# Sparse attention and soft mixture of experts on one core: order of layer 2's weight loads, of the coefficient transposes and of the output blocks changed

## The chip, the core and the metric

The kernel runs on one core of one Trainium2 chip. The metric is device microseconds of one execution. One core has five engines that run side by side: TensorE (PE, with its weight loads shown as PEld), VectorE (DVE), ScalarE (ACT), GpSimd (POOL) and SyncE (SP). Sixteen DMA engines move data between the chip's memory and the core; nearly all of their transfers are issued by SP's queue, in the order in which they are written.

## What is computed

Attention over 8 batches, 8 heads, 576 positions and 64 columns with two sparse masks gives tokens `x` of 4608 x 512. A soft mixture of 8 experts with 4 slots each follows:

```python
logits = x @ phi                                  # 4608 x 32
slot_input = softmax(logits, over tokens).T @ x   # 32 x 512
for e in range(8):
    h = np.maximum(slot_input[e] @ w1[e], 0.0)    # layer 1: 4 x 1024
    slot_out[e] = h @ w2[e]                       # layer 2: 4 x 512
c = softmax(logits, over slots)                   # the coefficients
out = c @ slot_out                                # 4608 x 512, f32, 9.4 MB
```

`w1` and `w2` are 16.8 MB each, in f32.

## The kernel before, in words

The attention and the slot sums fill the first 180 us, in an order written out by hand (`ORDER`); the change leaves that part as it is. What follows is layer 1, layer 2 and the output.

**Weights.** `load_weights` issues 64 loads of 512 KB on SP's queue. Number 0 to 31 are layer 1's. Layer 2's are 32 to 63, in pairs of a group of four experts and a quarter of the hidden size (`GM`). Pairs 0 to 5 (32 to 55) are loaded whole, four loads each, every partition reading 4 KB in one run. Pairs 6 and 7 are loaded in halves of the output columns: 56 to 59 hold their left halves, 60 to 63 their right halves, read in runs of 1 KB (the view `128x4x256`). `seq` is the order of issue. The late loads go into buffers of layer 1's weights that TensorE has finished with.

**Layer 1.** `emit_first` (steps P0 to P6 of `ORDER`) and `emit_end1` (step "e") multiply one group of four experts and a quarter of the input at a time. `COEFF` says which coefficient work follows a step: `emit_cT` and `emit_cU` are PE transposes of `lall`, `emit_cV` is ACT's copy back, `emit_cA`, `emit_cE` and `emit_cB` are the softmax on DVE and ACT. The nine blocks of tokens are in three sets (0 to 3, 4 to 6, 7 and 8).

**Layer 2 and output.** A string of letters, `SEQ`, sets the order of the rest on all engines. "h" turns the hidden rows (`emit_hT`). "l" adds one pair to the left sum (output columns 0 to 255), "r" one pair to the right sum (`emit_l2`): 8 matmuls, 16 passes. "s" copies a finished sum to `acc` (`emit_sg`: first DVE, then ACT), "t" adds it up over row groups (`emit_rs`: two matmuls and a copy each by DVE and ACT to `x9b`). "o" and "O" write two blocks of tokens in the left and the right half of the columns (`emit_half`: 8 matmuls, 4 copies, 4 stores of 256 KB in runs of 1 KB), "f" writes one block in all columns (`emit_full`, runs of 2 KB). Each of the three is 1.05 MB of output. An "o" needs the left sum, an "O" and an "f" both sums. Before, `SEQ` closes the left sum, starts the right one in the waits of "s" and "t", writes three left blocks between the other right pairs, and then, after the right sum, three right blocks and three whole ones.

Of the kernel before, what the change touches and what calls it, by code (L numbers as in the profile page):

```python
# [28 lines left out]
NWX = 2  # L29
# [49 lines left out]
s9w s9P sw w.14 ac1 zz.15 w.15 sP0 sD0 P0 sP1 sD1 P1 zD zP rg P2 P3 P4 P5 P6  # L79
""".split()  # L80

SEQ = "eehhllllllllsrtrorrorrorrstOOOfff"


def shape_constants():
# [23 lines left out]
def tile_sparse_attention_soft_moe(  # L109
# [107 lines left out]
    def take():  # L217
        x = min(freed, key=lambda x: freed[x])
        del freed[x]
        return banks[x], x  # L220
# [11 lines left out]
    order = wbufs + [t[:, 1024 * k:1024 * k + 1024] for t, k in places]  # L232

    NL = len(order)
    seq = list(range(32 - NWX)) + list(range(32, NL)) + list(range(32 - NWX, 32)) + list(range(NL, 64))
    wts = {}

    reuse = [x for x in range(32) if x not in (3, 4, 5)]
# [6 lines left out]
    def load_weights(n):  # L245
        for _ in range(n):
            if len(wts) >= 64:
                return
            j = seq[len(wts)]
            buf = order[len(wts)] if j < NL else wts[reuse[j - NL]]  # L250
            wts[j] = buf
            if j < 32:

                g, r = divmod(j, 16)
                c, e = divmod(r, 4)
                nc.sync.dma_start(out=buf, in_=w1[4 * g + e, 128 * CH[c]:128 * CH[c] + 128, :])
            else:
                r = j - 32
                if r < 4 * NG:
                    (g, m), e = GM[r // 4], r % 4  # L260
                    src = w2[4 * g + e, 256 * m:256 * m + 256, :].rearrange("(p j) d -> p (j d)", j=2)
                    nc.sync.dma_start(out=buf, in_=src)
                else:

                    x, r = divmod(r - 4 * NG, 16 - 2 * NG)
                    g, m = GM[NG + r // 2]
                    src = w2[4 * g:4 * g + 4, 256 * m:256 * m + 256].rearrange("e (p j) d -> j p e d", j=2)[r % 2, :, :, 256 * x:256 * x + 256]
                    nc.sync.dma_start(out=buf.rearrange("p (e d) -> p e d", d=256), in_=src)
# [428 lines left out]
    fns = {}  # L697
# [150 lines left out]
    def emit_l1(g, c, xs):  # L848
        for x in xs:
            for e in range(4):  # L850
# [3 lines left out]

    COEFF = {2: ((emit_cA, 0), (emit_cE, 0)),
             3: ((emit_cA, 1), (emit_cE, 1), (emit_cB, 0)),
             4: ((emit_cT, 2), (emit_cA, 2), (emit_cE, 2), (emit_cB, 1)),
             5: ((emit_cU, 0), (emit_cV, 0), (emit_cB, 2)),
             6: ((emit_cU, 1), (emit_cV, 1), (emit_cU, 2), (emit_cV, 2))}

    def emit_first(n):
        if n == 0:
            ph.append(take())
        emit_l1(n // 4, n % 4, (0, 1))
        load_weights((3, 2, 4, 4, 4, 1, 0)[n])

        for fn, x in COEFF.get(n, ()):
            fn(x)
        if n == 1:
            for t in hts:  # L870
                nc.gpsimd.memset(t, 0.0)
# [20 lines left out]
    for a in range(2):  # L892
        r = slice(64 - 64 * a, 128 - 64 * a)
# [23 lines left out]
    for x in ORDER:  # L917
        if x in once:
            once[x]()
        elif x[0] == "w":  # L920
            load_weights(1)
        else:
            n, i = x.split(".")
            i = int(i)
            if n == "C2":
                emit_late(i)
            fns[n](i)
# [24 lines left out]
    free = [wts[j] for j in list(range(22, 32)) + list(range(32, 48))]  # L952
    pos = [take() for x in range(2)]

    def emit_l2(x, n):
        g, m = GM[n]
        for j in range(2):
            for e in range(4):
                if n < NG:
                    w = wts[32 + 4 * n + e][:, 512 * j + 256 * x:512 * j + 256 * x + 256]  # L960
                else:
                    w = wts[32 + 4 * NG + (16 - 2 * NG) * x + 2 * (n - NG) + j][:, 256 * e:256 * e + 256]
                nc.tensor.matmul(out=pos[x][0][32 * e:32 * e + 32, 0:256], lhsT=hts[g][:, 2 * m + j, 32 * e:32 * e + 32], rhs=w,  # L963
                                 start=(n == 0 and j == 0), stop=(n == 7 and j == 1), skip_group_check=True)

    rss = [None, None]
    def emit_sg(x):
# [46 lines left out]
    def emit_full(vb):  # L1014
# [15 lines left out]
        emit_out(po, store)  # L1030


    steps = {
        "l": (emit_l2, 0, iter(range(8))), "r": (emit_l2, 1, iter(range(8))),
        "o": (emit_half, 0, iter(range(3))), "O": (emit_half, 1, iter(range(3))), "f": (emit_full, iter((8, 6, 7))),
        "s": (emit_sg, iter(range(2))), "t": (emit_rs, iter(range(2))), "h": (emit_hT, iter(range(2))),
        "e": (emit_end1, iter(range(2))),
    }
    for step in SEQ:
        fn, *args = steps[step]  # L1040
# [31 lines left out]
```

## Time and profile before

| | us |
|---|---|
| median of 3 runs (243.9 to 248.25) | 245.46 |
| the profiled execution | 242.59 |
| its span, first to last instruction | 240.8 |
| PE busy, share of the span | 89% |
| DMA queue of SP, share of 16 engines | 92.2% |

The profile shows one execution. PE is busy nearly throughout, and so are the DMA engines, so the shares alone don't tell the bound; the last 60 us have to be read stretch by stretch. In a row of stretches, PE to POOL are busy microseconds, then come TensorE's granted clock as a share of full speed, the mean busy share of the 16 DMA engines (packets can overlap, so it may pass 1) and what they moved in GB/s.

### The profile page before, as it was taken

Reading aid. Unit: us, or ns where it says so; the run is one execution under the profiler, and the core shown is the slowest. Engines: PE = TensorE matmul, PEld = TensorE weight load, DVE = VectorE, ACT = ScalarE, POOL = GpSimd, SP = SyncE. Lnnn points to the kernel's source line nnn. Section 1 sums busy time; section 2 is a strip of 40 time slices with the busy share of each in tenths; the row PEclk is TensorE's granted clock in tenths of the full one; section 3 lists DMA queues with packets and bytes.
Section 4 is the critical chain, followed back from the end, with each engine's and each line's share of the span. In section 5 each row is a group of like instructions: output and inputs, shape, how many; then the busy total and the mean of one; then the engine's idle time right before and its main releaser. Section 6 shows DMA issues by size and latency. Waiting matters only on the chain.

```text
span 240.8 us, 9926 instructions
## 1 busy us (share of the span) xinstructions
PE 215.2 (89%) x4096; PEld 169.0 (70%) x4096; DVE 165.6 (69%) x381; ACT 154.3 (64%) x347; POOL 86.0 (36%) x189
## 2 busy tenths in 40 slices
PE   8899998998889999999999999899889999998700
PEld 3688897888778998897889898687753246455400
DVE  6097997896599978887977786799872831145900
ACT  2789898786769889878697988666440241135700
POOL 5466835626443271743327434733102000000000
PEclk9999999999999999999999999999999999999975
DMA  5987999989997998899999899999998999887996
GB/s 151 351 231 238 301 282 279 302 207 318 304 321 218 299 317 236 263 344 297 318 367 340 233 280 335 316 284 358 349 344 338 395 377 312 293 287 257 381 399 260
DMA packets 69597, 72.73 MB, mean 302 GB/s; under 512 B 32896, under 2 KB 59664, under 8 KB 69552
## 3 DMA queue, kind: packets, MB, share of 16 engines
q1 hardware_dynamic: 69184, 71.84, 92.2%
q8 instruction: 32, 0.52, 0.9%
q0 software_dynamic: 80, 0.15, 0.2%
q10 hardware_dynamic: 288, 0.11, 0.2%
q14 instruction: 13, 0.11, 0.2%
HBM read 62.65 MB, written 9.44 MB: 299 GB/s over the span
## 4 chain that ended last, share of the span: by engine, by line
PE 54%; DMA 18%; DVE 13%; issue 4%; ACT 3%; POOL 2%; SPq 1%; DVEq 0%; POOLq 0%; ACTq 0%
PE bank L340 10%; PE bank L390 7%; PE bank L470 7%; DMA natb<-in_q_dram 6%; PE bank L851 6%; DMA vs<-in_v_dram 5%; PE bank L518 4%; DMA wb<-in_moe_w_dram 4%; PE bank L963 3%; PE bank L462 3%; PE bank L276 2%; PE bank L988 2%; DVE xnb L500 2%; DMA natb<-in_k_dram 2%; PE bank L549 2%
## 5 line engine op out<-in xcount | busy, mean ns | idle before, releaser
L340 PE MATMUL bank<-cf,natb 128*128 128x128 f32 x276 | 40.2, 277 | 3.0 <-DMA natb<-in_k_dram 1.3
L340 PEld LDWEIGHTS bank<-cf,natb 128*128 128x128 f32 x276 | 30.8, 141 | 8.0 <-issue 3.0
L356 ACT COPY kLb<-bank 64x256 f32<-64x256 f32 x64 | 25.8, 403 | 7.5 <-PE bank L340 4.7
L427 DVE TENSOR_TENSOR pb<-bank,cb 128x512 f32<-128x512 f32 (+2 forms) x48 | 21.7, 472 | 11.4 <-PE bank L390 7.4
L500 DVE TENSOR_TENSOR xnb<-bank,rz 128x512 f32<-128x512 f32 (+1 forms) x33 | 21.6, 669 | 7.6 <-PE bank L470 4.9
L330 POOL COPY vb<-vb 64x1024 f32<-64x1024 f32 x16 | 16.7, 1041 | 25.8 <-DMA vb<-in_v_dram 14.8
L390 PE MATMUL bank<-kLb,qtb 128*32 128x128 f32 x576 | 23.1, 274 | 0.8 <-POOL kLb L383 0.8
L442 DVE TENSOR_REDUCE rz<-pb 128x10 f32<-128x640 f32 (+1 forms) x32 | 21.6, 684 | 1.0 <-ACT pb L439 0.6
L466 ACT COPY ptb<-bank 128x512 f32<-128x512 f32 x32 | 19.0, 598 | 4.5 <-PE bank L462 2.9
L432 DVE TENSOR_REDUCE mx<-pb 128x10 f32<-128x640 f32 (+1 forms) x32 | 21.5, 685 | 0.5
L435 DVE TENSOR_TENSOR pb<-pb,mx 128x640 f32<-128x640 f32 (+1 forms) x32 | 21.1, 673 | 0.3
L439 ACT ACTIVATE pb<-pb 128x640 f32<-128x640 f32 (+1 forms) x32 | 18.6, 597 | 3.5 <-DVE pb L435 3.3
L335 POOL COPY natb<-natb 128x512 f32<-128x512 f32 x15 | 9.6, 638 | 30.1 <-DMA natb<-in_q_dram 18.9
L462 PE MATMUL bank<-cf,pb 128*128 128x128 f32 x128 | 19.4, 276 | 0.8 <-ACT d L619 0.7
L518 PE MATMUL bank<-cf,xnb 128*128 128x128 f32 x128 | 18.8, 277 | 0.7 <-DVE xnb L500 0.5
L390 PEld LDWEIGHTS bank<-kLb,qtb 128*32 128x32 f32 x576 | 17.1, 110 | 3.4 <-POOL kLb L383 1.5
L364 ACT COPY kSb<-bank 64x512 f32<-64x512 f32 x32 | 18.6, 581 | 0.4
L387 POOL COPY kSb<-qtb 64x32 f32<-64x32 f32 x64 | 17.5, 273 | 2.4
L470 PE MATMUL bank<-vs,ptb 128*32 128x128 f32 x480 | 16.0, 274 | 2.4 <-DMA vs<-in_v_dram 1.1
L470 PE MATMUL bank<-vb,ptb 128*32 128x128 f32 x512 | 17.4, 274 | 0.0
L331 POOL COPY vb<-vb 64x1024 f32<-64x1024 f32 x16 | 16.8, 1048 | 0.7
L518 PEld LDWEIGHTS bank<-cf,xnb 128*128 128x128 f32 x128 | 14.4, 141 | 2.6 <-issue 1.2
(199 smaller groups left out, 457.2 us busy)
## 6 DMA issues: line engine op xcount, KB each, us to landing
wb<-in_moe_w_dram SPq DMA_DIRECT2D x48, 512.0 KB
natb<-in_k_dram SPq DMA_DIRECT2D x30, 256.0 KB
natb<-in_q_dram SPq DMA_DIRECT2D x30, 256.0 KB
vb<-in_v_dram SPq DMA_DIRECT2D x32, 144.0 KB
vs<-in_v_dram SPq DMA_DIRECT2D x30, 144.0 KB
out_dram<-wb SPq DMA_DIRECT2D x16, 256.0 KB
vb<-in_moe_w_dram SPq DMA_DIRECT2D x4, 512.0 KB
xnb<-in_moe_w_dram SPq DMA_DIRECT2D x3, 512.0 KB
```

Of the source, the lines that this page charges most:

```text
L340: nc.tensor.transpose(out=t[0][:, 128 * n:128 * n + 128], in_=src[:, 128 * n:128 * n + 128], identity=ident)
L356: ACT(out=dst.rearrange("d (p j n) -> d p j n", j=2, n=2)[:, :, :, n], in_=t[0][64 * n:64 * n + 64].rearrange("d (h j p) -> d p j h", j=2, ...
L390: nc.tensor.matmul(out=t[0][32 * c:32 * c + 32, x:x + wd], lhsT=lhsT, rhs=rhs, start=True, stop=True, skip_group_check=True)
L427: nc.vector.tensor_tensor(out=dst, in0=src, in1=masks[w].unsqueeze(1).unsqueeze(3).to_broadcast([P, n, kk, 2]), op=ALU.add)
L432: nc.vector.tensor_reduce(out=part(box[i][0], w), in_=psg[w].rearrange("p s k a -> p s a k"), op=ALU.max, axis=AX.X)
L435: nc.vector.tensor_tensor(out=psg[w], in0=psg[w], in1=over(box[i][0], w), op=ALU.subtract)
L442: nc.vector.tensor_reduce(out=part(box[i][1], w), in_=psg[w].rearrange("p s k a -> p s a k"), op=ALU.add, axis=AX.X)
L462: nc.tensor.transpose(out=t[0][:, 128 * r:128 * r + 128], in_=pb[:, lo + 128 * r:lo + 128 * r + 128], identity=ident)
L466: ACT(out=ptL if s == "L" else ptS, in_=t[0])
L470: nc.tensor.matmul(out=t[0][32 * c:32 * c + 32, 128 * r:128 * r + 128], lhsT=lhsT, rhs=rhs, start=True, stop=True, skip_group_check=True)
L500: nc.vector.tensor_tensor(out=xn[:, place(i, s), r0:r0 + nr].rearrange("p r (a d) -> p r a d", a=2), in0=t[0][:, 128 * r0:128 * r0 + 128 * ...
L518: nc.tensor.transpose(out=t[0][:, 128 * r:128 * r + 128], in_=xn[:, place(i, s), r, :], identity=ident)
```

## The change

Five things change together. `seq` issues loads 56 to 59 (the left halves of pairs 6 and 7) ahead of 48 to 55 (the whole pairs 4 and 5); each load's buffer follows its place in the order. The left sum takes its pairs in the same order (`LEFT`), and closes with pair 5. The coefficient work of sets 1 and 2 leaves layer 1's steps P4 to P6 and stands in `SEQ` as "T" and "A" around the second "h", and as "U" and "V" around "t". The right sum no longer has pairs in the waits of "s" and "t"; the first "o" follows "V". And all blocks of tokens but the ninth are written in halves: four "o" between the right pairs, then four "O" and one "f".

```diff
--- before.py
+++ after.py
@@ -79,7 +79,7 @@
 s9w s9P sw w.14 ac1 zz.15 w.15 sP0 sD0 P0 sP1 sD1 P1 zD zP rg P2 P3 P4 P5 P6
 """.split()
 
-SEQ = "eehhllllllllsrtrorrorrorrstOOOfff"
+SEQ = "eehThAllllllllsUtVorrorrorrorrstOOOOf"
 
 
 def shape_constants():
@@ -232,7 +232,7 @@
     order = wbufs + [t[:, 1024 * k:1024 * k + 1024] for t, k in places]
 
     NL = len(order)
-    seq = list(range(32 - NWX)) + list(range(32, NL)) + list(range(32 - NWX, 32)) + list(range(NL, 64))
+    seq = list(range(32 - NWX)) + list(range(32, NL)) + list(range(32 - NWX, 32)) + list(range(NL, 48)) + list(range(56, 60)) + list(range(48, 56)) + list(range(60, 64))
     wts = {}
 
     reuse = [x for x in range(32) if x not in (3, 4, 5)]
@@ -246,8 +246,8 @@
         for _ in range(n):
             if len(wts) >= 64:
                 return
-            j = seq[len(wts)]
-            buf = order[len(wts)] if j < NL else wts[reuse[j - NL]]
+            j, n = seq[len(wts)], len(wts)
+            buf = order[n] if n < NL else wts[reuse[n - NL]]
             wts[j] = buf
             if j < 32:
 
@@ -854,9 +854,8 @@
 
     COEFF = {2: ((emit_cA, 0), (emit_cE, 0)),
              3: ((emit_cA, 1), (emit_cE, 1), (emit_cB, 0)),
-             4: ((emit_cT, 2), (emit_cA, 2), (emit_cE, 2), (emit_cB, 1)),
-             5: ((emit_cU, 0), (emit_cV, 0), (emit_cB, 2)),
-             6: ((emit_cU, 1), (emit_cV, 1), (emit_cU, 2), (emit_cV, 2))}
+             4: ((emit_cB, 1),),
+             5: ((emit_cU, 0), (emit_cV, 0))}
 
     def emit_first(n):
         if n == 0:
@@ -952,6 +951,9 @@
     free = [wts[j] for j in list(range(22, 32)) + list(range(32, 48))]
     pos = [take() for x in range(2)]
 
+    LEFT = (0, 1, 2, 3, 6, 7, 4, 5)
+    LAST = LEFT[-1], 7
+
     def emit_l2(x, n):
         g, m = GM[n]
         for j in range(2):
@@ -961,7 +963,7 @@
                 else:
                     w = wts[32 + 4 * NG + (16 - 2 * NG) * x + 2 * (n - NG) + j][:, 256 * e:256 * e + 256]
                 nc.tensor.matmul(out=pos[x][0][32 * e:32 * e + 32, 0:256], lhsT=hts[g][:, 2 * m + j, 32 * e:32 * e + 32], rhs=w,
-                                 start=(n == 0 and j == 0), stop=(n == 7 and j == 1), skip_group_check=True)
+                                 start=(n == 0 and j == 0), stop=(n == LAST[x] and j == 1), skip_group_check=True)
 
     rss = [None, None]
     def emit_sg(x):
@@ -1030,9 +1032,15 @@
         emit_out(po, store)
 
 
+    def emit_c(*fns):
+        for fn, x in fns:
+            fn(x)
+
     steps = {
-        "l": (emit_l2, 0, iter(range(8))), "r": (emit_l2, 1, iter(range(8))),
-        "o": (emit_half, 0, iter(range(3))), "O": (emit_half, 1, iter(range(3))), "f": (emit_full, iter((8, 6, 7))),
+        "T": (emit_c, (emit_cT, 2)), "A": (emit_c, (emit_cA, 2), (emit_cE, 2), (emit_cB, 2)),
+        "U": (emit_c, (emit_cU, 1), (emit_cV, 1)), "V": (emit_c, (emit_cU, 2), (emit_cV, 2)),
+        "l": (emit_l2, 0, iter(LEFT)), "r": (emit_l2, 1, iter(range(8))),
+        "o": (emit_half, 0, iter(range(4))), "O": (emit_half, 1, iter(range(4))), "f": (emit_full, iter((8,))),
         "s": (emit_sg, iter(range(2))), "t": (emit_rs, iter(range(2))), "h": (emit_hT, iter(range(2))),
         "e": (emit_end1, iter(range(2))),
     }
```

PE at the close of the left sum, before: the last two rows of the right sum's first half pair, then the sum over row groups (`acc` by `cf`), the second half pair, and the first left block (`x9b` by `lall`). Buffers `wb_92` and `wb_93` are the turned hidden rows, the other operand is a weight buffer.

```order
L963 MATMUL bank_119<-qtb,wb_92 32x256
L963 MATMUL bank_119<-vs,wb_92 32x256
L978 MATMUL bank_124<-acc,cf 128x128
L978 MATMUL bank_118<-acc,cf 128x128
L963 MATMUL bank_119<-vs,wb_93 32x256
L963 MATMUL bank_119<-vb,wb_93 32x256
L963 MATMUL bank_119<-natb,wb_93 32x256 x2
L963 MATMUL bank_119<-vs,wb_93 32x256
L963 MATMUL bank_119<-vb,wb_93 32x256
L963 MATMUL bank_119<-natb,wb_93 32x256 x2
L988 MATMUL bank_121<-x9b,lall 128x256
```

The same place now: the last rows of the left sum, then the coefficient transposes (`lall` by `cf`) on both sides of the sum over row groups, then the first left block.

```order
L965 MATMUL bank_120<-wb_102,wb_92 32x256
L965 MATMUL bank_120<-wb_103,wb_92 32x256
L965 MATMUL bank_120<-wb_104,wb_92 32x256
L833 MATMUL bank_123<-cf,lall 128x128 x3
L980 MATMUL bank_121<-acc,cf 128x128
L980 MATMUL bank_125<-acc,cf 128x128
L833 MATMUL bank_118<-cf,lall 128x128 x2
L990 MATMUL bank_119<-x9b,lall 128x256
```

Two pairs of the right sum have left this place; five transposes have come in, and the first left block stands directly behind them.

SP's queue, layer 2's last loads, as a difference: buffers 90 to 96 now take the left halves (1 KB runs), buffers 101 to 104 a whole pair (4 KB runs).

```order
-L262 DMA wb_90<-in_moe_w_dram 128x1024
-L262 DMA wb_94<-in_moe_w_dram 128x1024
-L262 DMA wb_95<-in_moe_w_dram 128x1024
-L262 DMA wb_96<-in_moe_w_dram 128x1024
+L268 DMA wb_90<-in_moe_w_dram 128x4x256
+L268 DMA wb_94<-in_moe_w_dram 128x4x256
+L268 DMA wb_95<-in_moe_w_dram 128x4x256
+L268 DMA wb_96<-in_moe_w_dram 128x4x256
 L262 DMA wb_97<-in_moe_w_dram 128x1024
 L262 DMA wb_98<-in_moe_w_dram 128x1024
 L262 DMA wb_99<-in_moe_w_dram 128x1024
 L262 DMA wb_100<-in_moe_w_dram 128x1024
```

The four small-run loads have moved ahead by eight places; behind them now come the two whole pairs, and behind those, as before, the right halves in `wb_105` to `wb_108`.

PE in layer 1, between step P6 and the last step, as a difference: five coefficient transposes are gone from here.

```order
 L851 MATMUL bank_125<-wb_114,pb 32x512
 L851 MATMUL bank_125<-wb_115,pb 32x512
-L833 MATMUL bank_124<-cf,lall 128x128 x3
-L833 MATMUL bank_118<-cf,lall 128x128 x2
 L851 MATMUL bank_121<-wb_116,pb 32x512
 L851 MATMUL bank_121<-wb_117,pb 32x512
```

Layer 1's last products now follow step P6 directly.

## Rows read from the trace of the kernel before

**Rows 1.** The page's first part: span, busy time of each engine

```profile
span 240.8 us, 9926 instructions
...
PE 215.2 (89%) x4096; PEld 169.0 (70%) x4096; DVE 165.6 (69%) x381; ACT 154.3 (64%) x347; POOL 86.0 (36%) x189
```

**Rows 2.** Busy time by stretch: us, PE, PEld, DVE, ACT, POOL, clock, DMA share, GB/s

```profile
184.00:196.90 12.90, 12.90 (x113) 4.15 (x109) 8.05 (x22) 2.92 (x7) 1.84 (x2) 1.00 1.02 399
196.90:203.00 6.10, 6.03 (x90) 3.48 (x85) 0.85 (x2) 2.11 (x4) 0.00 (x0) 1.00 1.03 326
203.00:206.20 3.20, 2.77 (x52) 1.42 (x44) 0.00 (x0) 0.00 (x0) 0.00 (x0) 1.00 0.99 258
```

**Rows 3.** Busy time by stretch, before and after the last left load's landing

```profile
196.90:206.20 9.30, 8.80 (x136) 4.90 (x128) 0.85 (x2) 2.11 (x4) 0.00 (x0) 1.00 1.01 302
206.20:212.10 5.90, 5.87 (x92) 3.28 (x92) 1.87 (x4) 1.61 (x4) 0.00 (x0) 1.00 0.69 237
```

**Rows 4.** Chain of work that ended last, in order of time: start, us, what

```profile
196.25 9.94 DMA wb<-in_moe_w_dram
...
206.23 1.50 PE bank L963 x24
...
209.38 1.08 PE bank L988 x16
210.45 1.86 PE bank L963 x32
...
216.33 1.91 PE bank L963 x32
218.26 0.30 DVE acc L969
...
219.43 0.28 ACT x9b L979
219.75 2.04 PE bank L988 x32
```

**Rows 5.** Order of time on PE: start, us, line, out<-in, count [idle before it]

```profile
190.32 0.44 PE L794 MATMUL bank<-cf,lall 128*128 128x128 f32 x2
...
192.54 0.66 PE L833 MATMUL bank<-cf,lall 128*128 128x128 f32 x4
...
194.98 0.76 PE L833 MATMUL bank<-cf,lall 128*128 128x128 f32 x5
...
199.08 0.40 PE L963 MATMUL bank<-kSb,wb 128*32 128x256 f32 x1
...
206.23 0.64 PE L963 MATMUL bank<-wb,wb 128*32 128x256 f32 x8 [0.47 <-DMA wb<-in_moe_w_dram]
...
209.31 1.15 PE L988 MATMUL bank<-x9b,lall 32*128 32x256 f32 x16
```

**Rows 6.** Busy time by stretch, from the weights' end to the span's end

```profile
209.00:212.10 3.10, 3.10 (x56) 1.66 (x48) 1.29 (x2) 1.07 (x2) 0.00 (x0) 1.00 0.40 140
...
221.00:222.60 1.60, 1.60 (x24) 0.94 (x20) 1.60 (x3) 1.60 (x4) 0.00 (x0) 1.00 0.01 3
222.60:231.20 8.60, 4.43 (x60) 2.99 (x56) 5.64 (x10) 4.71 (x9) 0.00 (x0) 1.00 1.09 382
231.20:238.40 7.20, 0.00 (x0) 0.00 (x0) 0.00 (x0) 0.00 (x0) 0.00 (x0) 0.51 1.06 406
238.40:240.80 2.40, 0.00 (x0) 0.00 (x0) 0.00 (x0) 0.00 (x0) 0.00 (x0) 0.50 0.11 40
```

**Rows 7.** Order of time on ACT: coefficient copies of sets 1 and 2

```profile
195.57 0.75 ACT L838 COPY lall<-bank 128x384 f32<-128x384 f32 x2 [1.75 <-PE bank L833]
```

**Rows 8.** Order of time on DVE: the first copy of the left sum

```profile
206.94 0.29 DVE L969 COPY acc<-bank 128x128 f32<-128x128 f32 x1 [7.25 <-PE bank L963]
```

**Rows 9.** Order of time on SP's queue: first store of the first left block

```profile
211.24 0.39 SPq L1010 DMA_DIRECT2D out_dram<-wb  x1
```

**Rows 10.** Order of time on SP's queue: first store after the right sum

```profile
221.69 0.37 SPq L1010 DMA_DIRECT2D out_dram<-wb  x1
```

## The prediction

> **What bounds the kernel now.** I read the page first: PE is busy for 215.2 of 240.8 us [rows 1], which only says that the last 60 us must be read by stretches. The chain of waits names who holds up the end. One piece of 9.94 us is a weight load that lands at 206.19; the left sum's last matmuls follow it, then the right sum and the left blocks, all on PE, and from 221.8 on copies and stores [rows 4]. Up to 206.2 the DMA engines never rest (share 1.02, 1.03, 0.99), and the loads get slower as their runs get shorter: 399 GB/s while nearly all are in 4 KB runs, then 326 and 258 while the eight loads in 1 KB runs are on their way [rows 2]. Behind the weights the stretches show two pauses: 209.0 to 212.1 with share 0.40 (1.9 us idle) and 221.0 to 222.6 with 0.01 (1.6 us). After 222.6 the stores run at 382 and 406 GB/s to 238.4, and 2.4 us at 40 GB/s end the span [rows 6].
>
> So three things stand in a row. The left sum closes by DMA: its last eight passes start on the landing and end at 206.23 + 0.64 = 206.87 [rows 5]. The right sum then closes by PE at 216.33 + 1.91 = 218.24 [rows 4]. From there the stores drain by DMA. The change touches all three, and I cost them one by one against this execution: span 240.8, time 242.59, so 1.8 around the span. The median of the runs shown is 245.46, 1.2% above it; I scale by that at the end.
>
> **The left sum's close.** In layer 1, transposes of 0.44 and 0.76 us leave PE (the four of 0.66 stay), and the 0.44 comes back as "T" between the two turns of the hidden rows. Layer 2, which starts at 199.08, can so start 0.8 sooner, at 198.3 [rows 5]. That alone gains nothing: PE already waits for the last load (0.47 idle, released by the DMA [rows 5]). But it sets a floor. Two pairs take 1.86 us [rows 4], so eight pairs take 7.44 and PE could close the left sum at 205.7 at the earliest. The DVE and ACT work of "A" (half a dozen operations) falls under layer 2, where DVE sits idle for 7.25 us [rows 8]; I cost it at nothing.
>
> The landing decides. Before and after, the same loads must land before the left sum closes, four of them in 1 KB runs; only their order differs, and the DMA engines are busy throughout, so by bytes nothing changes. Two bounds come from rows. For the better: after 206.2 the engines still moved 5.9 us x 237 GB/s = 1.40 MB [rows 3], although the four right halves are 2.10 MB. So 0.70 MB of these had moved before the last left load was complete, worth 2.3 us at 302 GB/s [rows 3]: the 16 engines are not in step. If they were, the landing would be at 203.9, and PE's floor of 205.7 would decide. For the worse: the small-run loads may run at 258 instead of 326 GB/s where they now stand, 2.10 MB x (1/258 - 1/326) = 1.7 us later. I take 0.7 us earlier, nearest to rows 2: the 3.2 us just before the landing ran at 258 instead of 326, which cost 3.2 x (1 - 258/326) = 0.7 us, and now 4 KB runs stand there, with the right halves behind them.
>
> The Trainium skill, "DMA: Bandwidth & Descriptors", section "Why a DMA increments its semaphore by 16 and not by 1", says that a transfer runs on up to 16 engines that finish independently, and that only the full count means all data has landed. By that the lag of the slowest engine stays whatever is queued, the landing moves by nothing and the sum below would give 242.5 instead of 241.8 (rival 3); the 0.70 MB that moved ahead of the landing agree with the page, while no row shows whether the lag shrinks under larger runs.
>
> After the landing there is a little more to do. A left half needs only its own 8 passes at the end (0.64 us [rows 5]). The last load of a whole pair serves both halves of the hidden rows, so its one matmul and the four of the second half follow: half a round of a pair more, at most 0.93/2, I take 0.4. The left sum closes at 206.87 - 0.7 + 0.4 = 206.6 (205.7 to 209.0).
>
> **From the left sum to the right sum.** Before, the first left block starts at 209.31 [rows 5], 2.4 us after the close, because two right pairs fill the waits. Without pairs the same waits are seen after the right sum: closed at 218.24, first block at 219.75, 1.5 us [rows 4]. Now U and V lie there: five transposes (0.76 us on PE [rows 5]) and two ACT copies (0.75 in all [rows 7]). The first block queues behind V on PE, and its `x9b` copy queues behind U's copy on ACT. In the 1.5 us PE waits for a DVE copy of 0.30 and an ACT copy of 0.28 [rows 4], and DVE's part of the work stays ahead of ACT's, so most of both fits beside them; I take 0.1 for what shows; the other end is all of it, 1.5. That gives 1.6. Then come four blocks of 1.08 and eight pairs of 0.93 [rows 4]: 4.3 + 7.4. The right sum closes at 206.6 + 1.6 + 11.8 = 219.9, 1.7 us later than before: a fourth block and two pairs that had filled waits now stand in its way.
>
> **The drain.** From the right sum's close to the first bytes of the next stores it takes 222.6 - 218.24 = 4.4 us [rows 4, 6], unchanged: 224.3. Then five blocks are left instead of six. A block is 1.05 MB: 2.75 us in 1 KB runs (382 GB/s), 2.58 in 2 KB runs (406) [rows 6]. Before: 3 x 2.75 + 3 x 2.58 = 16.0. Now 4 x 2.75 + 2.58 = 13.6, so 2.4 less. The end: 224.3 + 13.6 + 2.2 = 240.1, where the same sum for before gives 222.6 + 16.0 + 2.2 = 240.8. Net: -0.3 (close) + 2.0 (path to the right sum) - 2.4 (drain) = -0.7 us. 241.8 on this execution's scale, 0.3% less; 244.7 on the median's.
>
> The pauses go where this says. The first store follows the first left block by 211.24 - 209.31 = 1.9 us [rows 5, 9], so it is issued at 206.6 + 1.6 + 1.9 = 210.1 instead of 211.24, about when the weights run out: the first pause mostly closes. The second stays. Left blocks come every 1.86 + 1.08 = 2.94 us [rows 4], slower than the DMA takes them, so the fourth one's bytes end near 222.6 and the next start at 224.3. What is late next is the right sum, by PE alone.
>
> **The rivals.** (1) *The left sum closes as early as PE allows*, because the engines draw level under the 4 KB runs. For it: PE's floor of 205.7. Against it: nothing in the trace shows the lag shrinking. 0.9 us better than the forecast: 240.9, 243.8 on the median's scale. (2) *Slower: the small-run loads cost more ahead of the whole pairs.* They ran at 326 GB/s in one stretch and at 258 in the next [rows 2]; at 258 the left sum closes at 209.0 and all behind it moves: 244.2, 247.1 on the median's scale. It is slower than before once the close comes after 207.3. (3) *No change.* Either the engines stay as far out of step as 0.70 MB and the landing does not move, or U and V are not hidden and cost 0.8 instead of 0.1. Each takes the gain away: 242.5, or 245.4. The first store after the right sum (221.69 [rows 10]) would then come more than two us late, and eat the block saved. (4) *Both pauses close*: 1.9 + 1.6 = 3.5 us off, 239.1, or 241.9. Against it: the second pause hangs on PE, as above.
>
> **How the numbers follow.** The forecast's own case, a gain of 0 to 1.4 us, has 0.42 (244.0 to 245.5 on the median's scale). Rival 1 has 0.2, rival 2 0.2, rival 3 0.13, rival 4 0.05. The range leaves out rival 4's and rival 2's far ends and allows for runs that differ by a per cent: 242.0 to 247.4. About 2% (4.9 us) is what a measurement of this kernel can tell from no change. Closing both pauses would bring only 1.4%, so faster has 0.03; slower by as much needs twice the loss of rival 2, 0.04; within 2% 0.93.
>
> **What would show it.** In the changed kernel's profile: the landing that releases the left sum's last row near 205.5; the first left block on PE 1.6 us behind the left sum, the first store issued near 210; DMA share near 1 from 209 to 222 and a pause of one to two us before 224; the right sum closing near 219.9; 13.6 us of stores behind it. It is wrong if the landing has moved by over a microsecond either way, if the first block waits for ACT's copies, or if the second pause is gone.

## The result, and the profile after

The changed kernel takes 245.87 us (median of 20 runs, 242.71 to 249.81), the kernel before 243.41 (20 runs, 239.58 to 248.25). The ratio is 1.0117, with a 95% interval of 1.0071 to 1.0164: slower by 1.2%, some 2.8 us, and inside the 2% that I had called no change. The forecast was a gain of 0.3%. A ratio keeps only a kernel's runs within 1.5% of its fastest, here 14 and 10 of 20, and of the 12 runs of e3 and e7 below only 3 and 2; so the difference of the means over all runs, 1.8 us for this pair, stands beside the ratios.

That 245.87 us lies inside the forecast's range of 242.0 to 247.4 us is luck: the range was scaled from three runs of the kernel before with a median of 245.46, and over 20 runs that kernel has 243.41.

The profiled execution of the changed kernel took 243.26 us. Its page begins so (answers to [rows 1]):

```profile
span 241.5 us, 9922 instructions
...
PE 215.7 (89%) x4096; PEld 169.4 (70%) x4096; DVE 165.1 (68%) x381; ACT 154.4 (64%) x347; POOL 85.3 (35%) x189
```

Nothing has become busier. The order of time shows the stretch that did grow: PE around the last left load (columns as in [rows 5]).

```profile
196.27 0.40 PE L965 MATMUL bank<-kSb,wb 128*32 128x256 f32 x1
...
199.55 2.98 PE L965 MATMUL bank<-wb,wb 128*32 128x256 f32 x50
203.15 0.62 PE L965 MATMUL bank<-wb,wb 128*32 128x256 f32 x2 [0.63 <-DMA wb<-in_moe_w_dram]
204.39 0.62 PE L965 MATMUL bank<-wb,wb 128*32 128x256 f32 x2 [0.62 <-DMA wb<-in_moe_w_dram]
205.63 0.62 PE L965 MATMUL bank<-wb,wb 128*32 128x256 f32 x2 [0.62 <-DMA wb<-in_moe_w_dram]
206.86 1.05 PE L965 MATMUL bank<-wb,wb 128*32 128x256 f32 x10 [0.61 <-DMA wb<-in_moe_w_dram]
...
209.44 1.15 PE L990 MATMUL bank<-x9b,lall 32*128 32x256 f32 x16
```

PE waits for each of the last four loads before the left sum's close, 2.5 us in all, where it waited 0.47 us once before [rows 5]. The loads come 1.24 us apart, 524 KB in 1.24 us or 423 GB/s, so at this point they are fast. They are late because of something earlier.

The chain of work that ended last (start, us, what; answers to [rows 4]):

```profile
178.75 1.92 PE bank L851 x16
...
195.83 10.99 DMA wb<-in_moe_w_dram
...
206.86 1.05 PE bank L965 x10
207.91 0.48 PE bank L833 x3
...
209.44 1.15 PE bank L990 x16
210.58 1.86 PE bank L965 x32
...
219.40 1.91 PE bank L965 x32
221.33 0.30 DVE acc L971
...
222.50 0.28 ACT x9b L981
222.82 2.04 PE bank L990 x32
```

Its first row is layer 1's first products. The same row in the chain of the kernel before:

```profile
180.23 1.92 PE bank L851 x16
```

Executions differ by microseconds ahead of layer 1, which the change doesn't touch: layer 1 starts at 178.75 here and between 178.75 and 185.3 in the profiles of this study. So I count from it. The last left load lands at 195.83 + 10.99 = 206.82, 28.07 us after layer 1's start; before, at 206.19 - 180.23 = 25.96. It lands **2.1 us later**, where I forecast 0.7 us earlier. In two more profiles of each kernel (below) the landing comes 26.6 and 27.4 us after layer 1's start, and before 26.4 and 25.6: over three profiles it is 1.4 us later.

Busy time by stretch (columns as in [rows 2]):

```profile
185.00:191.00 6.00, 6.00 (x60) 1.85 (x48) 4.85 (x11) 1.15 (x2) 0.20 (x1) 1.00 0.84 221
191.00:203.00 12.00, 11.49 (x156) 5.76 (x154) 2.83 (x8) 3.12 (x6) 0.00 (x0) 1.00 1.03 405
203.00:209.00 6.00, 4.00 (x24) 1.81 (x25) 0.47 (x2) 0.65 (x2) 0.00 (x0) 1.00 0.97 338
209.00:214.00 5.00, 4.86 (x79) 2.82 (x81) 1.86 (x4) 2.08 (x5) 0.00 (x0) 1.00 0.35 120
214.00:224.00 10.00, 9.14 (x148) 5.54 (x144) 3.99 (x8) 3.33 (x8) 0.00 (x0) 1.00 1.06 371
224.00:225.60 1.60, 1.60 (x24) 0.93 (x20) 1.56 (x3) 1.58 (x4) 0.00 (x0) 1.00 0.20 69
225.60:239.60 14.00, 3.30 (x44) 2.19 (x40) 4.51 (x8) 3.70 (x7) 0.00 (x0) 0.71 1.05 374
```

The first row is where the four left halves, in 1 KB runs, now stand: share 0.84, 221 GB/s. Behind them the whole pairs run at 405. The same place in the kernel before, 6.3 us after layer 1's start, when whole pairs ran there:

```profile
186.50:192.50 6.00, 6.00 (x58) 1.53 (x46) 5.03 (x12) 1.57 (x3) 0.17 (x1) 1.00 1.00 392
```

So I split the end of every kernel in three: from layer 1's start to DVE's first copy of the left sum, from there to its first copy of the right sum, and from there to the span's end. Microseconds, from one profile each where no number stands in brackets:

| kernel | to left sum | to right sum | to the end | all | ratio to before, 95% | all runs, mean minus before's |
|---|---|---|---|---|---|---|
| before (mean of 3) | 26.7 (26.4 to 27.1) | 11.3 | 22.6 | 60.6 | | |
| after (mean of 3) | 28.5 (27.7 to 29.2) | 13.4 | 20.1 | 62.0 | 1.0117 (1.0071 to 1.0164) | +1.8 |
| e1 order only | 28.0 | 11.4 | 22.6 | 61.9 | 1.0144 (1.0085 to 1.0203) | +2.1 |
| e2 old order (2 profiles; ratio of the second) | 27.0, 26.9 | 13.4 | 20.1 | 60.5, 60.4 | 1.0053 (1.001 to 1.0095) | +1.0, +0.4 |
| e3 one pair later | 26.8 | 13.4 | 20.1 | 60.3 | 0.9938 (0.9872 to 1.0005) | +1.5 |
| e4 by expert | 26.0 | 13.4 | 20.1 | 59.5 | 1.0014 (0.9972 to 1.0057) | -0.7 |
| e5 old order, by expert | 25.6 | 13.4 | 20.1 | 59.1 | 1.0048 (0.9991 to 1.0106) | -1.0 |
| e6 long runs | 26.4 | 13.4 | 20.1 | 59.9 | 0.9973 (0.9928 to 1.0017) | -1.0 |
| e7 two right pairs early | 26.4 | 11.9 | 20.1 | 58.4 | 0.9845 (0.9749 to 0.994) | -1.2 |
| e8 small runs ahead | 28.6 | 13.4 | 20.1 | 62.2 | one run | |
| e9 the same, old order | 28.7 | 14.7 | 20.1 | 63.5 | one run | |

### The profile page after: what moved, and what is told of

It reads as the page before. It is cut to its first block, busy times and chain, and to the rows that moved or that the text cites. A ratio compares the mean times of both kernels' runs of the same rounds, so it can differ in the third digit from the quotient of the medians.

```text
span 241.5 us, 9922 instructions
## 1 busy us (share of the span) xinstructions
PE 215.7 (89%) x4096; PEld 169.4 (70%) x4096; DVE 165.1 (68%) x381; ACT 154.4 (64%) x347; POOL 85.3 (35%) x189
## 4 chain that ended last, share of the span: by engine, by line
PE 57%; DMA 18%; DVE 13%; ACT 3%; issue 2%; POOL 1%; SPq 1%; DVEq 0%; POOLq 0%; ACTq 0%
PE bank L340 11%; DMA wb<-in_moe_w_dram 9%; PE bank L470 8%; PE bank L390 8%; DMA natb<-in_q_dram 7%; PE bank L518 4%; PE bank L462 4%; PE bank L965 4%; PE bank L990 3%; PE bank L851 2%; PE bank L276 2%; PE bank L538 2%; PE bank L549 2%; DMA natb<-in_k_dram 2%; PE bank L669 2%
## 5 line engine op out<-in xcount | busy, mean ns | idle before, releaser
L435 DVE TENSOR_TENSOR pb<-pb,mx 128x640 f32<-128x640 f32 (+1 forms) x32 | 20.3, 646 | 0.3
L470 PE MATMUL bank<-vb,ptb 128*32 128x128 f32 x512 | 17.5, 274 | 0.2
```

Of the source, the lines that this page charges most:

```text
L435: nc.vector.tensor_tensor(out=psg[w], in0=psg[w], in1=over(box[i][0], w), op=ALU.subtract)
L470: nc.tensor.matmul(out=t[0][32 * c:32 * c + 32, 128 * r:128 * r + 128], lhsT=lhsT, rhs=rhs, start=True, stop=True, skip_group_check=True)
```

## The experiments

**Which part of the change loses it.** e1 has the new order of the loads alone, e2 all the rest with the old order.

```diff
 e1: kernel before
+seq = ... + list(range(NL, 48)) + list(range(56, 60)) + list(range(48, 56)) + list(range(60, 64))
+buf = order[n] if n < NL else wts[reuse[n - NL]]
+LEFT = (0, 1, 2, 3, 6, 7, 4, 5)
 e2: changed kernel
+seq = ... + list(range(NL, 64))
+LEFT = (0, 1, 2, 3, 4, 5, 6, 7)
```

> The kernel before with one part of the change alone: the left halves of pairs 6 and 7 loaded ahead of the whole pairs 4 and 5, and the left sum taking its pairs in that order. Theory A (the load order carries the loss: the four early small-run loads move at 170 to 260 GB/s instead of 326): the left sum closes about 2.5 us later after the start of layer 1 than before (29.2 instead of 26.6 us), everything behind it is unchanged, so 2.5 us slower, ratio 1.010. Theory B (the loss is on PE: the fourth left block and the two pairs that no longer fill the waits): none of it is in here, ratio 1.000 within 0.3%.

> The changed kernel with the load order and the order of the left sum as before; coefficient turns, four left blocks and the halves as changed. Theory A: the left sum closes at most 0.5 us away from before (26.2 to 27.1 us after layer 1's start), the path to the right sum is 2.0 us longer and the drain 2.4 us shorter, so 0.4 us faster than before, ratio 0.996 to 1.000. Theory B: the loss stays, ratio 1.008 to 1.014.

> The kernel with the old load order and all other parts of the change, once more, for an interval. Theory A: left sum closed 26.4 to 27.3 us after layer 1's start, ratio 0.995 to 1.003. Theory B (loss on PE): 1.008 or more.

e1's left sum comes 28.0 us after layer 1's start, its time rises by 1.4%. Its stretch with the left halves, 6.2 us after layer 1's start:

```profile
187.50:193.50 6.00, 6.00 (x58) 1.57 (x50) 5.00 (x13) 1.57 (x3) 0.25 (x1) 1.00 0.81 225
```

e2's left sum comes at 27.0 and 26.9 us, 0.2 to 0.3 later than the mean of before. Its median of 12 runs is 244.12 against 243.31. The order alone brings the loss. Whether the other four parts gain or cost is open: the profiles have 60.4 and 60.5 us against 60.6, but the ratio, 1.0053, lies above the 1.003 that I had expected at most.

**Is it chance?** Both kernels were profiled twice more.

> The kernel before, one more profiled execution, to see how far its own stretches repeat. If the one read for the prediction was typical, the left sum closes 26.2 to 27.2 us after layer 1's start and 60.1 to 61.1 us lie between that start and the end of the span. If it was an unlucky one, by 1 us or more less: the difference between the timed ratios and the profiles would then come from the profile of before.

> As b1: 26.2 to 27.2 us to the left sum's close if the first profile was typical.

> The changed kernel, one more profiled execution. If the slow early small-run loads are a property of the order, the left sum closes 28 to 30 us after layer 1's start again, and the 4 early loads move below 260 GB/s. If it was one execution's bad luck, 27 us or less.

> As a1: 28 to 30 us to the left sum's close if the slow loads belong to the order, 27 or less if they were bad luck.

The first two stretches, 6.2 us after layer 1's start, are those of a1 and a2 with the left halves, the third is that of b1 with whole pairs:

```profile
190.70:196.70 6.00, 6.00 (x60) 1.85 (x48) 4.86 (x11) 1.15 (x2) 0.18 (x1) 1.00 0.86 235
187.50:193.50 6.00, 6.00 (x60) 1.87 (x52) 4.88 (x12) 1.16 (x2) 0.23 (x1) 1.00 0.84 226
191.50:197.50 6.00, 6.00 (x58) 1.57 (x50) 5.00 (x13) 1.57 (x3) 0.24 (x1) 1.00 1.02 384
```

DVE's first copy of the left sum in b1, b2, a1 and a2, where layer 1 starts at 185.29, 181.67, 184.43 and 181.28:

```profile
212.40 0.29 DVE L969 COPY acc<-bank 128x128 f32<-128x128 f32 x1 [7.65 <-PE bank L963]
208.06 0.29 DVE L969 COPY acc<-bank 128x128 f32<-128x128 f32 x1 [6.94 <-PE bank L963]
212.11 0.29 DVE L971 COPY acc<-bank 128x128 f32<-128x128 f32 x1 [7.04 <-PE bank L965]
209.84 0.29 DVE L971 COPY acc<-bank 128x128 f32<-128x128 f32 x1 [7.91 <-PE bank L965]
```

To the left sum: before 26.7, 27.1 and 26.4, after 29.2, 27.7 and 28.6. They don't overlap, and the means differ by 1.7 us (before rounding). One of the three, 27.7, is below the 28 that I had expected at least. The whole, 60.6 and 62.0, differs by 1.4 us.

**Is it the run length, or the place?** In e6 the loads of pairs 6 and 7 read other rows in 4 KB runs, at the same places in the queue and with as many bytes.

```diff
-src = w2[4 * g:4 * g + 4, ...].rearrange("e (p j) d -> j p e d", j=2)[r % 2, :, :, 256 * x:256 * x + 256]
+src = w2[4 * g + 2 * x + r % 2, 256 * m:256 * m + 256, :].rearrange("(p j) d -> p (j d)", j=2)
```

> The changed kernel with pairs 6 and 7 read from other rows of layer 2's weights, in 4 KB runs instead of 1 KB (so these two pairs are multiplied with the wrong rows: the kernel measures the run length alone, with order, buffers and bytes as changed). Theory A (the small runs cost about 3.5 us in their early place, all of it ahead of the left sum): loads go on at 400 GB/s, the left sum closes at 25.0 to 26.0 us after layer 1's start instead of 29.2, three to four us faster than the changed kernel, ratio to before 0.985 to 0.995. Theory C (what slows the loads there is the company: layer 1's and the coefficients' work): the stretch stays below 300 GB/s with 4 KB runs too, and the left sum closes at 28 us or later, ratio 1.005 or more.

The stretch 6.2 us after layer 1's start in e6:

```profile
185.70:191.70 6.00, 6.00 (x60) 1.87 (x52) 4.89 (x12) 1.15 (x2) 0.24 (x1) 1.00 1.01 382
```

382 GB/s instead of 221, and the left sum at 26.4 instead of 28.5: with long runs the loads stay fast in this place. The left sum is no earlier than the earliest of before's, and the ratio, 0.9973 (0.9928 to 1.0017), is not the gain that I expected: no gain clear of the scatter comes from moving the loads forward, even when they are cheap.

**Does the price belong to the place, or to the first loads in short runs?** In e8 one more pair, the one directly ahead of the left halves (pair 3), is read in 1 KB runs (of the edit, the new source is shown).

```diff
+if r // 4 == 3:
+    src = w2[4 * g:4 * g + 4, ...].rearrange("e (p j) d -> j p e d", j=2)[e % 2, :, :, 256 * (e // 2):256 * (e // 2) + 256]
```

> The changed kernel with pair 3, the loads just ahead of the early left halves, read in 1 KB runs as well (so pair 3 is multiplied with other rows of layer 2's weights). The early left halves stand in the same place and the same company as in the changed kernel. If the first small-run loads after long runs pay and the next run freely, the four left halves now move at 340 GB/s or more (6 us or less from the last load ahead of them to the fourth one's median landing, instead of 8.9). If layer 1's work beside them slows small runs, they take 8 us or more again.

Two stretches of e8: the last two loads of pair 3, then the four left halves.

```profile
183.80:188.20 4.40, 4.40 (x45) 1.39 (x49) 3.98 (x12) 1.15 (x2) 1.69 (x2) 1.00 0.89 204
188.20:193.80 5.60, 5.60 (x56) 1.83 (x52) 2.09 (x5) 0.59 (x1) 0.00 (x0) 1.00 1.07 364
```

Now pair 3's last two loads pay, at 204 GB/s, and the left halves run at 364, in the same place of the queue and beside the same layer 1 on PE. So neither their own shape nor layer 1 as company is enough: the same four loads are slow or fast by what stands ahead of them. The left sum, at 28.6 us, gains nothing, since pair 3's price lies ahead of it as well.

That it is the first loads in short runs that pay is not shown. SP's queue in e8 (L263 is pair 3, L256 layer 1's last two loads, in 4 KB runs), and the stretch in which pair 3's first two loads land:

```profile
169.93 1.23 SPq L263 DMA_DIRECT2D xnb<-in_moe_w_dram  x1
174.87 0.38 SPq L263 DMA_DIRECT2D xtb<-in_moe_w_dram  x1
177.45 0.81 SPq L256 DMA_DIRECT2D xnb<-in_moe_w_dram  x2
180.97 0.93 SPq L263 DMA_DIRECT2D wb<-in_moe_w_dram  x2
...
176.60:179.80 3.20, 2.37 (x30) 1.22 (x26) 1.98 (x8) 0.20 (x1) 0.00 (x0) 1.00 0.95 299
```

The first two loads in short runs move at 299 GB/s, and it is the third and the fourth, behind two loads in long runs, that move at 204. So here it is not the first loads in short runs that pay most. A rival that no run isolates is how much stands queued when such a load is issued: from issue to median landing the first two left halves take 6.1 and 7.1 us in the changed kernel, 7.6 and 7.4 in e8, and 9.7 and 8.6 before.

e9 does the same with the old order, where four whole loads of pair 4 and four of pair 5 stand between pair 3 and the left halves.

> Old load order with the other parts of the change, and pair 3 in 1 KB runs as above. If the price is paid once, by the first small-run loads, and stays paid through the eight 4 KB loads between, the eight last small-run loads take 11.0 to 11.6 us instead of 13.3, and the left sum closes 26.5 us or less after layer 1's start. If every change from long to small runs pays anew, they take 13 us or more again.

Pair 3's first two loads, its last two, the left halves, and the stretch in which the right halves begin:

```profile
180.00:183.60 3.60, 2.78 (x32) 1.59 (x36) 2.41 (x10) 0.59 (x3) 0.00 (x0) 1.00 0.93 232
188.00:192.20 4.20, 4.20 (x44) 1.30 (x40) 3.94 (x11) 1.16 (x2) 1.36 (x2) 1.00 0.87 243
202.20:206.20 4.00, 3.95 (x76) 2.12 (x68) 1.22 (x4) 0.01 (x1) 0.00 (x0) 1.00 1.07 382
206.20:210.40 4.20, 1.59 (x24) 0.31 (x16) 0.00 (x0) 0.00 (x0) 0.00 (x0) 1.00 0.97 297
```

Here both parts of pair 3 are slow (232 and 243), so the second pays again, two long loads behind the first. The left halves pay no more (382), though eight long loads lie between. A slow patch at the right halves stays (297), which the expectation did not have, and the left sum, at 28.7, came later than expected, since pair 3's own price lies ahead of it. What sets the second patch is open. The 1.3 us more to the right sum (14.7 in the table) are TensorE's: busy for 1.9 us of the five from 206 to 211, it then had a granted clock of 0.50 (1.2 GHz) from 212 to 214:

```profile
212.00:213.00 1.00, 1.00 (x5) 1.00 (x6) 0.29 (x1) 0.53 (x2) 0.00 (x0) 0.50 1.03 354
```

**Does a smaller price ahead of the sum show?** In e3 the left halves move by one pair less. In e4 and e5 each of the loads becomes two, one for each expert; a partition's runs of 1 KB then lie 2 KB apart instead of 2 MB (1024 x 512 words of four bytes). e4 has the new order, e5 the old. (The old lines that these replace, and the index of the weight in layer 2's matmul, which follows, are left out.)

```diff
 e3:
+seq = ... + list(range(NL, 52)) + list(range(56, 60)) + list(range(52, 56)) + list(range(60, 64))
+LEFT = (0, 1, 2, 3, 4, 6, 7, 5)
 e4, e5:
+for k in range(2):
+    src = w2[4 * g + 2 * (r % 2) + k, 256 * m:256 * m + 256].rearrange("(p j) d -> p j d", j=2)[:, :, 256 * x:256 * x + 256]
+    nc.sync.dma_start(out=buf[:, 512 * k:512 * k + 512].rearrange("p (j d) -> p j d", j=2), in_=src)
```

> The changed kernel with the four small-run loads one pair later: pair 4, then the left halves, then pair 5. If the small runs are slow because of what else goes on in their place, some 5 us further on (the start of layer 1), they move at 300 GB/s or more here, the left sum closes within 1 us of before and the ratio is 0.997 to 1.004. If they are slow wherever 4 KB loads follow them, they stay near 230 GB/s, the left sum closes 2.5 us late, ratio 1.010.

> The changed kernel with another shape of the eight small-run loads: each 512 KB as two transfers of one expert each, so that a partition's two 1 KB runs lie 2 KB apart, where before its four runs lay 2 MB apart. Same place, same bytes, same run length. If the 2 MB steps make the small runs slow, the early ones move at 330 GB/s or more and the late ones too, the left sum closes 2 to 3 us earlier than in the changed kernel, ratio to before 0.997 or less. If only the run length or the place matters, nothing changes: ratio 1.012, the early ones near 230 GB/s.

> Old load order, the other parts of the change, and the eight small-run loads as transfers of one expert each. If these lose less than the runs 2 MB apart (1.9 instead of 2.6 us in all), the left sum closes near 26.0 us after layer 1's start and the kernel is 0.5 to 1 us faster than before, ratio 0.995 to 1.000. If the shape does not matter, as the old order alone: 26.4 to 27.3 us, ratio 0.998 to 1.003.

e3, ahead of the left halves and at them:

```profile
185.10:190.50 5.40, 5.40 (x56) 1.44 (x46) 4.86 (x11) 1.15 (x2) 0.21 (x1) 1.00 1.00 395
190.60:195.60 5.00, 4.97 (x45) 2.03 (x42) 0.00 (x0) 1.91 (x3) 0.00 (x0) 1.00 0.87 249
```

e4, in the place where the changed kernel had 221 GB/s:

```profile
187.20:193.20 6.00, 6.00 (x60) 1.85 (x48) 4.86 (x11) 1.15 (x2) 0.19 (x1) 1.00 0.96 300
```

In e3 the slow stretch moves along with the loads (249). Its left sum comes at 26.8, as before's, but its runs scatter from 239.61 to 248.79 us, and the table's ratio and difference of means have opposite signs: inconclusive, and neither expectation came true as a whole. e4 runs at 300 instead of 221, and its left sum comes at 26.0 instead of 28.5. e5, with the old order, has the earliest left sum of all, 25.6. So the shape of the transfer carries much of the price (each load is also two transfers now, and no run parts the two). With this shape the order hardly matters: 25.6 and 26.0, one profile each, are closer than three profiles of one kernel. The timed runs don't confirm a gain over the kernel before: ratios of 1.0014 and 1.0048, both above what I had expected, and means 0.7 and 1.0 us below.

The Trainium skill, "DMA: Bandwidth & Descriptors", section "Latency and other measured facts", reports copies between memory tensors at 164 GB/s where the rows of neighbouring partitions lie 2 MiB apart, against 207 at 512 KiB, and names, as an unverified inference, streams in step that meet in the same memory channel. In this kernel the step of 2 MB lies between the runs of one partition, a case that it does not report. 221 GB/s at 2 MB and 300 at 2 KB agree with it in sign; e8's 364 GB/s at the same step does not, so such a step is not the whole cause.

**Two right pairs ahead of the last left one.** e7 is e5 with two right pairs ahead of the last left pair, and one pair less between the third and the fourth left block.

```diff
-SEQ = "eehThAllllllllsUtVorrorrorrorrstOOOOf"
+SEQ = "eehThAlllllllrrlsUtVorrorrororstOOOOf"
```

> As the one before, with two right pairs ahead of the last left pair, where PE would wait for its load, and the fourth left block one right pair earlier. If the time from the left to the right sum is PE's alone, as the prediction had it, that takes 1.9 us off it (11.5 instead of 13.4), and the whole is 1.5 to 2 us faster than with the pairs behind, ratio to before 0.988 to 0.994. If the two pairs hold up the left sum, it closes 1 us or more later and nothing is gained, ratio 0.998 or more.

DVE's first copies of both sums in e7:

```profile
209.22 0.29 DVE L972 COPY acc<-bank 128x128 f32<-128x128 f32 x1 [5.78 <-PE bank L966]
...
221.09 0.28 DVE L972 COPY acc<-bank 128x128 f32<-128x128 f32 x1
```

The left sum comes 0.9 us later than in e5, the right sum 221.09 - 209.22 = 11.9 us behind it instead of 13.4: 0.7 us gained, 58.4 in all, the least of the table. Its ratio, 0.9845 with an interval of 0.9749 to 0.994, is the lowest, but stands on two of its 12 runs, and the 12 scatter from 236.68 to 249.87. The median of all 12 is 242.24 against 243.31 for before, 0.4% less; the profile's own gain, 60.6 - 58.4 = 2.2 us, is 0.9%. Against the changed kernel it is ahead by every measure (62.0 to 58.4 us in the profiles, and -1.2 against +1.8 us in the means over all runs); whether it gains on the kernel before, and how much, stays uncertain.

## Why the prediction was wrong, step by step

**The landing: wrong, and all of the miss.** The step is "I take 0.7 us earlier, nearest to rows 2". It came 2.1 us later in this profile, beyond the worse bound of 1.7 that the same paragraph worked out, and 1.4 us later over three profiles of each, inside it: 2.1 us from the forecast. So the sign that I had named for being wrong is there, a landing moved by over a microsecond. I treated the short runs' slowness as a rate that stays with the place in the order, and put long runs there. Rival 2 named what happened, "the small-run loads cost more ahead of the whole pairs", and its price, 244.2 - 242.59 = 1.6 us, is close to the 1.4 us of the table. The rate at the new place is 221 GB/s, lower than both rates that I had from before (326 and 258 [rows 2]), and e6 shows that with 4 KB runs it isn't slow there at all. The sentence "by bytes nothing changes" is true, and missed that the time of the loads can change with what stands ahead of them.

Where the price stood before can be worked out from the landing records (us, from one load's landing to the next, each taken as the median over the 16 engines):

```
                            first two left halves      a normal one
kernel before, 3 profiles   2.0 1.5 / 2.0 1.8 / 1.9 1.4      1.35
after, 3 profiles           2.6 2.9 / 2.6 2.6 / 2.5 3.5      1.35
```

Before, the first two left halves lose 0.6 to 1.1 us in all, and the first two right halves (2.2 and 1.9 us in the profiled execution) 1.4 us more, behind the left sum, which doesn't wait for them. The changed order loses 2.5 to 3.3 us ahead of the left sum, and its right halves, now behind eight loads in long runs, lose next to nothing (1.4 us each for the first three in the profiled execution). Of the 2.1 us more at the left halves (means 2.9 and 0.8), 1.4 arrive at the last landing: the eight whole loads take 10.1 us instead of 10.5, and the last engine trails the median by 2.3 us instead of 2.7. The half round of matmuls behind the landing, forecast at 0.4 us, adds 0.4, which makes some 1.7 us at the close. What the change moved was where a price is paid, and it put nearly all of it ahead of the one wait that sets the path. Why these loads pay is not shown.

The Trainium skill, "DMA: Bandwidth & Descriptors", section "Why a DMA increments its semaphore by 16 and not by 1", counts engines that finish independently. The landing records agree: in the changed kernel's profile the 16 engines finish a load 0.7 to 2.6 us apart in the seven loads up to the first left half, and 3.5 to 4.9 from the second left half on, through the 4 KB loads that follow; before, 1.0 to 2.7 through the whole loads and 3.7 at the last left half. That the lag stays whatever is queued was my inference; this section does not say so. In the profiled executions it nearly did (the last engine trails the median by 2.8 us before and 3.1 after, at the last landing ahead of the left sum), but rival 3's outcome, a landing that doesn't move, fell all the same, because the median itself came later.

**The floor and "A": right in sign.** Layer 2 starts 196.27 - 178.75 = 17.5 us after layer 1, and before 199.08 - 180.23 = 18.9 [rows 5]: 1.3 sooner, 0.8 forecast. No wait for DVE's work of "A" shows on the path. As said, it gains nothing by itself.

**From the left sum to the right sum: right.** From the close, 207.91, to the first left block, 209.44, are 1.53 us (1.6 forecast); U and V are hidden, so that half of rival 3 falls. From close to close it takes 221.31 - 207.91 = 13.4 (1.6 + 11.8 = 13.4).

**The drain: right.** From the right sum's close, 219.40 + 1.91 = 221.31, to the span's end are 20.2 us (4.4 + 13.6 + 2.2 = 20.2).

**The pauses: half right.** The second stays, 224.0 to 225.6 at share 0.20. The first was to close "mostly", with the first store near 210.1. It was issued at 211.32, because the left sum closed late:

```profile
211.32 11.36 SPq L1012 DMA_DIRECT2D out_dram<-wb  x16
```

From 209 to 214 the share is 0.35: some 3.2 us idle, where the first pause before had 1.9, so it has grown. Rivals 1 and 4 fall: PE's floor of 205.7 was never reached, as each of the last four loads was waited for.

**The sum.** With the close 28.5 us after layer 1's start instead of 26.7, and the other terms as forecast, the change is +1.7 + 2.1 - 2.4 = +1.4 us (means before rounding), and the profiles' 62.0 against 60.6 say the same. (The prediction's own sum, 242.59 - 0.7, is 241.9; it wrote 241.8.) The ratio's 2.8 us (1.7 to 4.0) is more. The means over all runs give 1.8. The rest is within what executions differ by ahead of layer 1, and I can't put it to any stretch.

## What to carry to other kernels

A load's duration can depend on what stands ahead of it in the queue, so bytes over a rate read elsewhere is no price for a load that is moved: look for a row that shows loads of its shape in the new place, or run that order alone first. When a sum of terms is made, the term with the widest bounds decides the sign; here it was a landing taken at a small gain with no row that showed the loads in their new place. And where pieces can be read so that a partition's runs lie close together, try that too: here it gave the earlier left sums of e4 and e5, in one profile each.

## What the runs showed of the hardware that I had not expected

The same four loads of 1 KB runs moved at 221 GB/s behind long runs and at 364 in the same place of the queue behind other 1 KB runs (e8); with eight long loads between, the left halves ran at 382 (e9). But in e8 the price fell on the third and fourth load in short runs more than on the first two (204 against 299 GB/s), so a rule of first loads does not cover all runs. The mean share of the 16 engines falls to 0.81 to 0.89 in the slow stretches of the early short runs, although loads had been issued (in e8 both of pair 3's last two by 181.9), and is 0.93 to 1.07 in the other stretches shown while weights load; but the patch at the right halves in e9 (297 GB/s, share 0.97) and the last stretch ahead of the landing before (258 GB/s, share 0.99 [rows 2]) were slow with busy engines, so idle engines are not all of it. Why some of these loads pay, and why the patch at the right halves remains in e9, no run here settles.
